# Attention and a gated MLP in one kernel: the weights' decode in 1024-column tiles with two VectorE steps, q and k in one tile of four column blocks

## The chip, the cores and the metric

The kernel runs on one core of a Trainium2 chip. A core has five engines that work side by side, each through its own queue in order: TensorE (PE, with its weight loads as PEld), VectorE (DVE), ScalarE (ACT), GpSimd (POOL) and SyncE (SP), which here only issues DMAs. SBUF is the on-chip memory with 128 partitions, PSUM the small one that TensorE writes. The metric is the device time of the program in microseconds; the kernel before was run three times, and the median counts.

## The reference, cut to what matters

```python
# q, k, v: (8, 8, 576, 64) fp32; moe weights: float64
scores = 1/sqrt(D) * q @ k.T            # a query block of 64 sees the key blocks up to its own
attn   = softmax(scores)
out    = attn @ v                       # -> x: (4608, 512), heads side by side
a = x @ w1;  b = x @ w2                 # (512, 1024) each
h = (a * b) @ w3                        # (1024, 1024)
return (h @ w_out).astype(np.float32)   # (1024, 512)
```

The four weight matrices arrive as 64-bit floats, q, k and v as 32-bit floats.

## The kernel before

The work is cut into 32 pairs of heads (8 batches with 4 pairs each, `pair(n)`, L427), each with two heads j. The matrices w3 and w_out are multiplied into one on the chip first, so that the MLP is two products, w1 and w2, a product of their results, and one more matmul. To keep fp32 accuracy at the speed of the faster 32-bit matmul format (`F32R`, a rounded float32), numbers are split into a rounded high part and a low part, and products are done in several passes: `w1h`/`w1l`, `w2h`/`w2l`, `wh`/`wl`, `xh`/`xl`, `gh`/`gl`, and for q and k `hi`/`lo`.

The program has an early stage and a late one. In the early stage the first four pairs (`EARLY`) do their attention while the weights are loaded, decoded and prepared (`gen_w`, L342). When both are done, the early pool of memory is closed and the late one opened (L480 to L486), and from there the order of TensorE's instructions is the order of the code (L488): pair 4 and the following, with MLP matmuls (`gen_moe`, L376) filled in between by the table `PLAN`. In the early stage a scheduler orders the instructions of each engine; attention's steps have the higher priority, and the letters of `EARLY_PLAN` say in which order the program offers them: S a tile of scores and its exp, V a part of the product with v, M a step of the next pair's row maximum (`shift_mask`), A and B steps of the preparation of q and k (`prep_qk`) for the next head or the own second head, N and T the end of a head and of a pair, Q the load of a later pair, and C one step of the weight generator. There are 40 C steps in the four pairs.

The decode (`load_w`, L122) turns 64-bit floats into 32-bit floats by integer arithmetic on the two 32-bit halves of each number. It works on 512 numbers per partition at a time: a DMA of 512 KB into `wraw` (5 buffers, issued on SP's queue, L130); ScalarE takes the absolute value of the high half, read with a step of two words (L135); then VectorE does four steps into `wbits` (6 buffers): a maximum (L136), a shift with a mask (L137), both on one tensor, the sign and top exponent bit merged in from the high half (L138), and the low half's top three bits merged in (L141). L138 and L141 read two tensors, one of them with a step of two words, and L141 keeps `wraw` in use to the end. There are 40 such tiles: 8 of w_out, 16 of w3 (in four-row pieces of 1 KB per partition), 8 of w1 and 8 of w2. For w1 and w2, ScalarE then rounds the result to the high part (L147) and GpSimd subtracts it for the low part (L148).

For the scores, q and k of a head are rounded on ScalarE in the early stage, on VectorE later (`cast`, L207). Two DMAs copy rounded blocks to the other 64 partitions (L209, L210), and GpSimd makes two differences of 64x576: k's low part (L211) and q's low part (L213). `lo` also holds constant rows for the mask, cast once at the start (L102), and a row of negated row maxima that a DMA writes (`shift`, L198). A score tile is two matmuls, one with `hi`, one with `lo` (L235), added up in PSUM.

Of the kernel before, what the change touches and what calls it, by code (L numbers as in the profile page):

```python
# [58 lines left out]
def block_causal_attention__then__gated_mlp_kernel(ctx, tc, qkv, consts, ident_in, w1, w2, w3t, wout, out_t):  # L59
# [43 lines left out]
    nc.gpsimd.memset(qd, 0.0)

    tl = {}
# [13 lines left out]
        tl["gh"] = pool.tile([P, NF, HALF], F32R, name="gh")  # L119
        tl["gl"] = pool.tile([P, NF, HALF], F32R, name="gl")  # L120

    def load_w(dst, src, k):  # L122

        t = tl["early"].tile([P, 1024], F32, tag="wraw", name="wraw", bufs=5)
        u = tl["early"].tile([P, 512], F32, tag="wbits", name="wbits", bufs=6)
        wide = t.bitcast(I32)
        nc.sync.dma_start(out=wide.rearrange("p (k w) -> p k w", k=k), in_=src)  # L130
# [4 lines left out]
        nc.scalar.activation(u, high.bitcast(F32), AF.Abs)  # L135
        V.tensor_scalar(out=u, in0=u, scalar1=2.0**-15, scalar2=None, op0=ALU.max)  # L136
        V.tensor_scalar(out=bits, in0=bits, scalar1=3, scalar2=0x3FFFFFF8, op0=ALU.logical_shift_left, op1=ALU.bitwise_and)  # L137
        V.scalar_tensor_tensor(out=bits, in0=high, scalar=-0x40000000, in1=bits, op0=ALU.bitwise_and, op1=ALU.bitwise_or)  # L138
        if dst is None:
            dst = u.unsqueeze(1)  # L140
        V.scalar_tensor_tensor(out=dst.bitcast(I32), in0=low.rearrange("p (k w) -> p k w", k=k), scalar=29,  # L141
                               in1=bits.rearrange("p (k w) -> p k w", k=k), op0=ALU.logical_shift_right, op1=ALU.bitwise_or)
        return u

    def load_split(dst_h, dst_l, src):
        val = load_w(None, src.unsqueeze(1), 1)
        nc.scalar.copy(dst_h, val)  # L147
        nc.gpsimd.tensor_tensor(out=dst_l, in0=val, in1=dst_h, op=ALU.subtract)  # L148

    def load_rows(dst_h, dst_l, src, c):  # L150
        for h in range(2):
            cs = slice(h * 512, (h + 1) * 512)
            load_split(dst_h[:, c, cs], dst_l[:, c, cs], src[c * P : (c + 1) * P, h * 1024 : (h + 1) * 1024])
            yield

    def cast(n, dst, src, act):
# [39 lines left out]
        yield  # L196

    def shift(n, j):  # L198
        row = lo[j][oth[j].start : oth[j].start + 1, 0, :].rearrange("p (i r) -> p i r", r=BLK)
        queue(n).dma_start(out=row.bitcast(F32), in_=ms_of[n][0:NB, j * BLK : (j + 1) * BLK].bitcast(F32))  # L200

    def prep_qk(n, j):
        rqk = raw_of[n][:, 0 : 2 * S].rearrange("p (t s) -> p t s", t=2)
        o, x = own[j], oth[j]
        if j == 1:
            shift(n, 1)
        cast(n, hi[j][o], rqk[o], CAST[0])  # L207
# [3 lines left out]
        nc.gpsimd.tensor_tensor(out=hi[j][x, 1, :], in0=rqk[o, 1, :], in1=hi[j][o, 1, :], op=ALU.subtract)  # L211
        yield
        nc.gpsimd.tensor_tensor(out=lo[j][o, 0, :], in0=rqk[o, 0, :], in1=hi[j][o, 0, :], op=ALU.subtract)  # L213
# [14 lines left out]
    def s_tile(n, j, parts, p_early):  # L228
# [3 lines left out]
        for c, q0, q1, e0 in parts:  # L232
            kr = slice(c * P, min((c + 1) * P, S))
            ks = slice(0, kr.stop - kr.start)
            for s, src in enumerate((hi[j], lo[j])):  # L235
                nc.tensor.matmul(t[ks, at : at + q1 - q0], src[:, 1, kr], src[:, 0, q0:q1], start=(s == 0), stop=(s == 1))  # L236
# [104 lines left out]

    def gen_w(wp):  # L342
        wo = tl["wo"]
        for k in range(NF):
            load_w(wo[:, k : k + 1, :], wout[k * P : (k + 1) * P, :].unsqueeze(1), 1)
            yield
        rows1 = (None for c in range(NC) for _ in load_rows(w1h, w1l, w1, c))
        pending = []

        def evacuate():  # L350
            m, acc = pending.pop(0)
            nc.scalar.copy(wh[:, m, :], acc)
            nc.vector.tensor_tensor(out=wl[:, m, :], in0=acc, in1=wh[:, m, :], op=ALU.subtract)

        for m in range(NF):
            t3 = wp.tile([P, NF, P], F32, tag="w3", name="w3", bufs=2)
            for k in range(0, NF, 4):
                src = w3t[k * P : (k + 4) * P, 2 * m * P : 2 * (m + 1) * P].rearrange("(k p) f -> p k f", p=P)
                load_w(t3[:, k : k + 4, :], src, 4)
                if k == 0:  # L360
                    yield
# [137 lines left out]
def _layout(q, k, v, moe_w1, moe_w2, moe_w3, moe_w_out):  # L499
    import numpy as np  # L500

    def heads_t(a):
# [9 lines left out]
    for c in range(4):  # L512
# [6 lines left out]
        "w1": np.ascontiguousarray(moe_w1).view(np.int64),  # L519
        "w2": np.ascontiguousarray(moe_w2).view(np.int64),  # L520
        "w3t": np.ascontiguousarray(moe_w3.T).view(np.int64),
        "wout": np.ascontiguousarray(moe_w_out).view(np.int64),
    }


# [17 lines left out]
```

## Time and profile before

| | us |
|---|---|
| three runs, median | 1022.3 |
| lowest and highest | 1020.81, 1022.79 |
| span of the profiled execution | 1019.4 |
| TensorE busy in the span | 965.8 |
| VectorE busy | 744.7 |
| GpSimd busy | 596.6 |
| ScalarE busy | 547.4 |

The span is the profiled execution's time from its first to its last instruction; what a timed run has beside it is the difference of 2.9 us between span and median. The page shows the span in 40 slices of 25.5 us with the busy share of each engine in tenths. Rows of instructions name line, engine, operation, the tile written and read, the shape, the count, then the busy time and the mean duration in ns of one, and behind the second bar the engine's idle time before them with what ended it. The row of a line or tile alone gives shortest, median and longest duration in ns.

### The profile page before, as it was taken

Reading aid. Unit: us, or ns where it says so; the run is one execution under the profiler, and the core shown is the slowest. Engines: PE = TensorE matmul, PEld = TensorE weight load, DVE = VectorE, ACT = ScalarE, POOL = GpSimd, SP = SyncE. Lnnn points to the kernel's source line nnn. Section 1 sums busy time; section 2 is a strip of 40 time slices with the busy share of each in tenths; the row PEclk is TensorE's granted clock in tenths of the full one; section 3 lists DMA queues with packets and bytes.
Section 4 is the critical chain, followed back from the end, with each engine's and each line's share of the span. In section 5 each row is a group of like instructions: output and inputs, shape, how many; then the busy total and the mean of one; then the engine's idle time right before and its main releaser. Section 6 shows DMA issues by size and latency. Waiting matters only on the chain.

```text
span 1019.4 us, 18475 instructions
## 1 busy us (share of the span) xinstructions
PE 965.8 (95%) x6594; PEld 888.3 (87%) x6624; DVE 744.7 (73%) x1320; ACT 547.4 (54%) x1433; POOL 596.6 (59%) x625
## 2 busy tenths in 40 slices
PE   3878878999999999999999999999999999999998
PEld 1444346999999999999999999999999999999998
DVE  7899886777787777777777778777777777775100
ACT  3645555656555555555565655555555556553221
POOL 3242466667676666767576767666675757673211
PEclk9889897999999999999999999999999999999999
DMA  8566542122212222222212221222222221110000
GB/s 299 170 205 196 172 122 59 49 83 61 61 51 69 73 60 73 66 78 61 84 49 84 61 66 46 70 72 64 69 67 78 60 85 48 48 25 25 1 24 24
DMA packets 37436, 80.42 MB, mean 79 GB/s; under 512 B 5408, under 2 KB 21920, under 8 KB 37344
## 3 DMA queue, kind: packets, MB, share of 16 engines
q1 hardware_dynamic: 35564, 76.26, 24.5%
q10 hardware_dynamic: 1780, 2.97, 1.2%
q8 instruction: 52, 0.85, 0.4%
q14 instruction: 40, 0.33, 0.1%
HBM read 50.76 MB, written 9.44 MB: 59 GB/s over the span
## 4 chain that ended last, share of the span: by engine, by line
PE 67%; DVE 16%; ACT 8%; issue 4%; DMA 4%; SPq 0%; ACTq 0%; POOL 0%; DVEq 0%; POOLq 0%
PE ab L387 28%; PE o L403 20%; PE s L236 7%; PE x L291 6%; DVE pl L254 5%; PE mx L183 3%; ACT ph L252 2%; ACT p L251 2%; DVE g L394 2%; PE x L275 1%; DVE wbits L138 1%; DMA wraw<-in_w 1%; DMA wraw<-in_w3t 1%; DVE wbits L136 1%; DVE x L329 1%
## 5 line engine op out<-in xcount | busy, mean ns | idle before, releaser
L257 POOL TENSOR_TENSOR rsum<-rsum,p 128x448 f32<-128x448 f32 x224 | 176.7, 789 | 108.4 <-ACT p L251 98.6
L254 DVE TENSOR_TENSOR pl<-p,ph 128x448 fp32r<-128x448 f32 x168 | 148.3, 896 | 60.1 <-ACT ph L252 59.2
L396 POOL TENSOR_TENSOR gl<-g,gh 128x288 fp32r<-128x288 f32 x128 | 107.5, 840 | 120.1 <-ACT gh L395 118.7
L395 ACT CAST gh<-g 128x288 fp32r<-128x288 f32 x128 | 55.5, 433 | 217.1 <-DVE g L394 217.1
L387 PE MATMUL ab<-xh,w2h 128*128 128x288 f32 x512 | 154.4, 301 | 0.0
L403 PE MATMUL o<-gh,wh 128*128 128x288 f32 x512 | 153.7, 300 | 0.0
L387 PE MATMUL ab<-xh,w1h 128*128 128x288 f32 x512 | 151.7, 296 | 1.6 <-ACT xh L338 1.6
L387 PE MATMUL ab<-xl,w2h 128*128 128x288 f32 x512 | 151.8, 296 | 0.0
L387 PE MATMUL ab<-xl,w1h 128*128 128x288 f32 x512 | 151.4, 296 | 0.3 <-POOL xl L339 0.3
L387 PE MATMUL ab<-xh,w2l 128*128 128x288 f32 x512 | 151.7, 296 | 0.0
L387 PE MATMUL ab<-xh,w1l 128*128 128x288 f32 x512 | 151.4, 296 | 0.0
L403 PE MATMUL o<-gl,wh 128*128 128x288 f32 x512 | 151.1, 295 | 0.0
L403 PE MATMUL o<-gh,wl 128*128 128x288 f32 x512 | 151.0, 295 | 0.0
L187 DVE TENSOR_REDUCE m<-mx 128x1 f32<-128x512 f32 (+6 forms) x320 | 128.7, 449 | 19.3 <-PE mx L183 17.4
L252 ACT ACTIVATE ph<-s 128x288 fp32r<-128x288 f32 x336 | 131.3, 393 | 0.8 <-issue 0.8
L236 PE MATMUL s<-hi 128*128 128x288 f32 (+4 forms) x384 | 123.0, 332 | 6.8 <-ACT pe L244 4.0
L211 POOL TENSOR_TENSOR hi<-raw,hi 64x576 fp32r<-64x576 f32 x64 | 92.9, 1451 | 33.3 <-ACT hi L157 16.4
L254 DVE TENSOR_TENSOR pl<-rsum,ph 128x288 fp32r<-128x288 f32 x112 | 74.6, 685 | 49.0 <-ACT ph L252 48.8
L251 ACT ACTIVATE p<-s 128x448 f32<-128x448 f32 x224 | 85.4, 381 | 46.3 <-PE s L236 43.3
L236 PE MATMUL s<-lo 128*128 128x288 f32 (+4 forms) x384 | 106.8, 306 | 3.4 <-issue 2.5
L394 DVE TENSOR_TENSOR g<-ab,a 128x288 f32<-128x288 f32 x128 | 57.7, 451 | 71.3 <-PE ab L387 63.3
L291 PE MATMUL x<-ph,vs 128*128 128x128 f32 x336 | 104.2, 320 | 0.0
(73 smaller groups left out, 2418.1 us busy)
## 6 DMA issues: line engine op xcount, KB each, us to landing
raw<-in_qkv SPq DMA_DIRECT2D x32, 896.0 KB
out_t<-o SPq DMA_DIRECT2D x64, 144.0 KB
wraw<-in_w3t SPq DMA_DIRECT2D x16, 512.0 KB
wraw<-in_w SPq DMA_DIRECT2D x16, 512.0 KB
hi<-hi SPq DMA_DIRECT2D x54, 144.0 KB
lo<-hi SPq DMA_DIRECT2D x54, 144.0 KB
wraw<-in_wout SPq DMA_DIRECT2D x8, 512.0 KB
hi<-hi ACTq DMA_DIRECT2D x10, 144.0 KB
```

What stands on the lines that cost most here:

```text
L187: nc.vector.reduce_max(m[:, col : col + 1], sc, axis=AX.X)
L211: nc.gpsimd.tensor_tensor(out=hi[j][x, 1, :], in0=rqk[o, 1, :], in1=hi[j][o, 1, :], op=ALU.subtract)
L236: nc.tensor.matmul(t[ks, at : at + q1 - q0], src[:, 1, kr], src[:, 0, q0:q1], start=(s == 0), stop=(s == 1))
L251: nc.scalar.activation(p32, t[ks, at : at + w], AF.Exp, scale=SCALE)
L252: nc.scalar.activation(ph[ks, o : o + w], t[ks, at : at + w], AF.Exp, scale=SCALE)
L254: nc.vector.tensor_tensor(out=low, in0=p32, in1=ph[ks, o : o + w], op=ALU.subtract)
L257: nc.gpsimd.tensor_tensor(out=r, in0=r, in1=p32, op=ALU.add)
L291: nc.tensor.matmul(xps[:, to : to + w], v[:, c, :], pr[:, a : a + w], start=(u < 2 and s == 0), stop=(u in (0, len(PV) - 1) and s == len(p ...
L387: nc.tensor.matmul(t[:, 0:HALF], l[:, c, fs], r, start=(c == 0 and s == 0), stop=(c == NC - 1 and s == 2))
L394: nc.vector.tensor_tensor(out=g32, in0=acc[1][:, 0:HALF], in1=a32, op=ALU.mult)
L396: nc.gpsimd.tensor_tensor(out=gl[:, f, :], in0=g32, in1=gh[:, f, :], op=ALU.subtract)
L403: nc.tensor.matmul(t[:, 0:HALF], l[:, f, es], r[:, f, :], start=(f == 0 and s == 0), stop=(f == NF - 1 and s == 2))
```

## The change

Three things are altered.

The weights are rearranged on the host so that every load is one whole tile of 1024 numbers per partition, 1 MB in one contiguous piece per partition. The 40 tiles become 20, the C steps of the table 20 instead of 40. `wraw`, the new `wy` and `wbits` have two buffers each. The decode is now: ScalarE multiplies the high half by a power of two (L134), GpSimd makes the low half's top three bits from byte 3 of each number, read as an 8-bit integer with a step of eight bytes and written as int32 (L135), and VectorE merges the sign into that (L136) and then the shifted value of ScalarE (L137). Both VectorE steps read two dense tensors, and neither reads `wraw`.

q and k of a head live in one tile `qk` of four column blocks: rounded q, rounded k, low q, low k on the head's own partitions, and constants, copied k, copied q, constants on the others. One difference of 64x1152 gives both low parts. It is on VectorE in the early stage and on GpSimd once the late pool is open. The score's two matmuls take blocks 1 and 2, then blocks 3 and 0. The two DMA copies remain.

The first load of q, k and v is cut into three DMAs, k first.

```diff
 EARLY_PLAN = (
-    "M S S S C S C C C C M S V V B C M M V A V M V M Q B M A B M N",
-    "S C C S A S S C S C V V V V V Q N T",
+    "M S S S C S C M S V V B C M M V A V M V M Q B M A B M N",
+    "S C S A S S C S V V V V V Q N T",
 )
...
-    hi = [cpool.tile([P, 2, S], F32R, name=f"hi{j}") for j in range(2)]
-    lo = [cpool.tile([P, 2, S], F32R, name=f"lo{j}") for j in range(2)]
+    qk = [cpool.tile([P, 4, S], F32R, name=f"qk{j}") for j in range(2)]
...
-        nc.sync.dma_start(out=t, in_=qkv[n // NPAIR, n % NPAIR])
+        src = qkv[n // NPAIR, n % NPAIR]
+        for cs in (slice(S, 2 * S), slice(0, S), slice(2 * S, RAW)) if n == 0 else (slice(0, RAW),):
+            nc.sync.dma_start(out=t[:, cs], in_=src[:, cs])
...
-    def load_w(dst, src, k):
-        t = tl["early"].tile([P, 1024], F32, tag="wraw", name="wraw", bufs=5)
-        u = tl["early"].tile([P, 512], F32, tag="wbits", name="wbits", bufs=6)
-        wide = t.bitcast(I32)
-        nc.sync.dma_start(out=wide.rearrange("p (k w) -> p k w", k=k), in_=src)
...
-        nc.scalar.activation(u, high.bitcast(F32), AF.Abs)
-        V.tensor_scalar(out=u, in0=u, scalar1=2.0**-15, scalar2=None, op0=ALU.max)
-        V.tensor_scalar(out=bits, in0=bits, scalar1=3, scalar2=0x3FFFFFF8, op0=ALU.logical_shift_left, op1=ALU.bitwise_and)
-        V.scalar_tensor_tensor(out=bits, in0=high, scalar=-0x40000000, in1=bits, op0=ALU.bitwise_and, op1=ALU.bitwise_or)
...
-        V.scalar_tensor_tensor(out=dst.bitcast(I32), in0=low.rearrange("p (k w) -> p k w", k=k), scalar=29,
-                               in1=bits.rearrange("p (k w) -> p k w", k=k), op0=ALU.logical_shift_right, op1=ALU.bitwise_or)
+    def load_w(dst, src):
+        t = tl["early"].tile([P, 2048], I32, tag="wraw", name="wraw", bufs=2)
+        y = tl["early"].tile([P, 1024], F32, tag="wy", name="wy", bufs=2)
+        bits = tl["early"].tile([P, 1024], I32, tag="wbits", name="wbits", bufs=2)
+        nc.sync.dma_start(out=t, in_=src)
+        high = t.rearrange("p (c two) -> p c two", two=2)[:, :, 1]
+        byte3 = t.bitcast(U8).rearrange("p (c e) -> p c e", e=8)[:, :, 3]
...
+        nc.scalar.mul(out=y, in_=high.bitcast(F32), mul=2.0**-112)
+        nc.gpsimd.tensor_scalar(out=bits, in0=byte3, scalar1=1.0 / 32, scalar2=-31.0 / 64, op0=ALU.mult, op1=ALU.add)
+        V.scalar_tensor_tensor(out=bits, in0=y.bitcast(I32), scalar=-0x80000000, in1=bits, op0=ALU.bitwise_and, op1=ALU.bitwise_or)
+        V.scalar_tensor_tensor(out=dst.bitcast(I32), in0=y.bitcast(I32), scalar=3, in1=bits, op0=ALU.logical_shift_left, op1=ALU.bitwise_or)
...
-        cast(n, hi[j][o], rqk[o], CAST[0])
+        cast(n, qk[j][o, 0:2], rqk[o], CAST[0])
         yield
-        queue(n).dma_start(out=hi[j][x, 0, :].bitcast(F32), in_=hi[j][o, 0, :].bitcast(F32))
-        queue(n).dma_start(out=lo[j][o, 1, :].bitcast(F32), in_=hi[j][o, 1, :].bitcast(F32))
-        nc.gpsimd.tensor_tensor(out=hi[j][x, 1, :], in0=rqk[o, 1, :], in1=hi[j][o, 1, :], op=ALU.subtract)
+        queue(n).dma_start(out=qk[j][x, 1, :].bitcast(F32), in_=qk[j][o, 1, :].bitcast(F32))
+        queue(n).dma_start(out=qk[j][x, 2, :].bitcast(F32), in_=qk[j][o, 0, :].bitcast(F32))
         yield
-        nc.gpsimd.tensor_tensor(out=lo[j][o, 0, :], in0=rqk[o, 0, :], in1=hi[j][o, 0, :], op=ALU.subtract)
+        (nc.gpsimd if "late" in tl else nc.vector).tensor_tensor(out=qk[j][o, 2:4], in0=rqk[o], in1=qk[j][o, 0:2], op=ALU.subtract)
         yield
...
-            for s, src in enumerate((hi[j], lo[j])):
-                nc.tensor.matmul(t[ks, at : at + q1 - q0], src[:, 1, kr], src[:, 0, q0:q1], start=(s == 0), stop=(s == 1))
+            for s, (k, q) in enumerate(((1, 2), (3, 0))):
+                nc.tensor.matmul(t[ks, at : at + q1 - q0], qk[j][:, k, kr], qk[j][:, q, q0:q1], start=(s == 0), stop=(s == 1))
```

How the rows of two engines stand before and now. First VectorE at the first tiles of w3 in the early stage (before; `w` is the decoded tile of w3; `rr` and `rb` belong to the end of pair 0):

```order
L138 SCALAR_TENSOR_TENSOR wbits<-wraw,wbits 128x512
L326 RECIPROCAL rr_154<-rr_154 128x18
L141 SCALAR_TENSOR_TENSOR w_321<-wraw,wbits 128x512
L328 STREAM_TRANSPOSE rb_368<-rr_154 128x576
L137 TENSOR_SCALAR wbits<-wbits 128x512
L136 TENSOR_SCALAR wbits<-wbits 128x512
L138 SCALAR_TENSOR_TENSOR wbits<-wraw,wbits 128x512
L137 TENSOR_SCALAR wbits<-wbits 128x512
L141 SCALAR_TENSOR_TENSOR wbits<-wraw,wbits 128x512
```

and now, at the same tiles (`m` are the row maxima of a later pair):

```order
L136 SCALAR_TENSOR_TENSOR wbits<-wy,wbits 128x1024
L180 TENSOR_TENSOR m_192<-m_192 128x1
L137 SCALAR_TENSOR_TENSOR w_286<-wy,wbits 128x1024
L136 SCALAR_TENSOR_TENSOR wbits<-wy,wbits 128x1024
L178 TENSOR_REDUCE m_390<-mx_0_391 128x1
L137 SCALAR_TENSOR_TENSOR w_356<-wy,wbits 128x1024
L136 SCALAR_TENSOR_TENSOR wbits<-wy,wbits 128x1024
L137 SCALAR_TENSOR_TENSOR wy<-wy,wbits 128x1024
L203 TENSOR_TENSOR qk_85<-raw_150,qk_85 64x1152
```

Eight steps of 512 columns have become two of twice the length for each 1024 numbers, and the difference of q and k (L203) now stands in this queue. Second GpSimd from its first work on data (before):

```order
L211 TENSOR_TENSOR hi_84<-raw_91,hi_84 64x576
L213 TENSOR_TENSOR lo_86<-raw_91,hi_84 64x576
L213 TENSOR_TENSOR lo_87<-raw_91,hi_85 64x576
L211 TENSOR_TENSOR hi_85<-raw_91,hi_85 64x576
L211 TENSOR_TENSOR hi_84<-raw_151,hi_84 64x576
L213 TENSOR_TENSOR lo_86<-raw_151,hi_84 64x576
L329 TENSOR_TENSOR x_0_153<-x_0_153,rb_368 128x576
```

and now:

```order
L135 TENSOR_SCALAR wbits<-wraw 128x1024 x8
L144 TENSOR_TENSOR w1l<-wy,w1h 128x1024
L135 TENSOR_SCALAR wbits<-wraw 128x1024
L319 TENSOR_TENSOR x_0_152<-x_0_152,rb_325 128x576
L135 TENSOR_SCALAR wbits<-wraw 128x1024
L329 TENSOR_TENSOR xl_0_329<-x_0_152,xh_0_328 128x288
```

The q/k differences have left GpSimd's queue in the early stage, and the byte steps of the weights, 20 in all, stand in their place; eight of them come ahead of its first other work.

More of the change, by code (lines that the diff above doesn't have):

```diff
@@ L11 @@
 I32 = mybir.dt.int32
+U8 = mybir.dt.uint8
 AF = mybir.ActivationFunctionType
@@ L101, in block_causal_attention__then__gated_mlp_kernel @@
     for j in range(2):
-        nc.vector.tensor_copy(lo[j][oth[j]], cst[0:D, 0 : 2 * S].rearrange("p (t s) -> p t s", t=2))
+        nc.vector.tensor_copy(qk[j][oth[j], 0:4:3, :], cst[0:D, 0 : 2 * S].rearrange("p (t s) -> p t s", t=2))
     nc.gpsimd.memset(qd, 0.0)
@@ L120, in open_late @@
         tl["gl"] = pool.tile([P, NF, HALF], F32R, name="gl")
-    def load_w(dst, src, k):
-        t = tl["early"].tile([P, 1024], F32, tag="wraw", name="wraw", bufs=5)
-        u = tl["early"].tile([P, 512], F32, tag="wbits", name="wbits", bufs=6)
-        wide = t.bitcast(I32)
-        nc.sync.dma_start(out=wide.rearrange("p (k w) -> p k w", k=k), in_=src)
-        wide = wide.rearrange("p (c two) -> p c two", two=2)
-        low, high = wide[:, :, 0], wide[:, :, 1]
-        bits = u.bitcast(I32)
-        V = nc.vector
[L135 to L141, printed above, removed]
-                               in1=bits.rearrange("p (k w) -> p k w", k=k), op0=ALU.logical_shift_right, op1=ALU.bitwise_or)
-        return u
@@ L145, in load_split @@
[L145 to L153, printed above, removed]
+    def load_w(dst, src):
[5 more added lines that the diff above has]
+        byte3 = t.bitcast(U8).rearrange("p (c e) -> p c e", e=8)[:, :, 3]
+        if dst is None:
+            dst = y
+        V = nc.vector
+        nc.scalar.mul(out=y, in_=high.bitcast(F32), mul=2.0**-112)
+        nc.gpsimd.tensor_scalar(out=bits, in0=byte3, scalar1=1.0 / 32, scalar2=-31.0 / 64, op0=ALU.mult, op1=ALU.add)
+        V.scalar_tensor_tensor(out=bits, in0=y.bitcast(I32), scalar=-0x80000000, in1=bits, op0=ALU.bitwise_and, op1=ALU.bitwise_or)
+        V.scalar_tensor_tensor(out=dst.bitcast(I32), in0=y.bitcast(I32), scalar=3, in1=bits, op0=ALU.logical_shift_left, op1=ALU.bitwise_or)
+        return y
@@ L154, in load_rows @@
+    def load_rows(dst_h, dst_l, src):
+        for c in range(NC):
+            val = load_w(None, src[c])
+            nc.scalar.copy(dst_h[:, c, :], val)
+            nc.gpsimd.tensor_tensor(out=dst_l[:, c, :], in0=val, in1=dst_h[:, c, :], op=ALU.subtract)
             yield
@@ L198, in shift @@
     def shift(n, j):
-        row = lo[j][oth[j].start : oth[j].start + 1, 0, :].rearrange("p (i r) -> p i r", r=BLK)
+        row = qk[j][oth[j].start : oth[j].start + 1, 0, :].rearrange("p (i r) -> p i r", r=BLK)
         queue(n).dma_start(out=row.bitcast(F32), in_=ms_of[n][0:NB, j * BLK : (j + 1) * BLK].bitcast(F32))
@@ L343, in gen_w @@
         wo = tl["wo"]
-        for k in range(NF):
-            load_w(wo[:, k : k + 1, :], wout[k * P : (k + 1) * P, :].unsqueeze(1), 1)
+        for u in range(NF // 2):
+            load_w(wo[:, 2 * u : 2 * u + 2, :].rearrange("p k w -> p (k w)"), wout[u])
             yield
-        rows1 = (None for c in range(NC) for _ in load_rows(w1h, w1l, w1, c))
+        rows1 = load_rows(w1h, w1l, w1)
         pending = []
@@ L356, in gen_w @@
             t3 = wp.tile([P, NF, P], F32, tag="w3", name="w3", bufs=2)
[L357 to L361, printed above, removed]
+            load_w(t3.rearrange("p k f -> p (k f)"), w3t[m])
             acc = ps_m.tile([P, 512], F32, tag="psm", name=f"w{m}")
@@ L368, in gen_w @@
             yield
-            next(rows1)
-            yield
+            if m % 2:
+                next(rows1)
+                yield
         while pending:
             evacuate()
-        for c in range(NC):
-            yield from load_rows(w2h, w2l, w2, c)
+        yield from load_rows(w2h, w2l, w2)
     def gen_moe(b):
@@ L503, in heads_t, with units @@
         return a.transpose(0, 1, 3, 2).reshape(B, NPAIR, P, S)
+    def units(w):
+        return np.ascontiguousarray(w).view(np.int64).reshape(-1, P, 1024)
     vp = np.zeros((B, NPAIR, P, 2, 5, D), v.dtype)
@@ L518, in _layout @@
         "ident": np.concatenate([np.eye(P), np.tile(np.eye(32), (4, 4))], axis=1).astype(np.float32),
[L519 to L522, printed above, removed]
+        "w1": units(moe_w1.reshape(NC, P, DF)),
+        "w2": units(moe_w2.reshape(NC, P, DF)),
+        "w3t": units(moe_w3.reshape(NF, P, NF, P).transpose(0, 3, 2, 1)),
+        "wout": units(moe_w_out.reshape(NF // 2, 2, P, DM).transpose(0, 2, 1, 3)),
     }
```

## The prediction

> **What bounds the kernel now.** I read first the slices of the page, then the busy time by stage. The page's rows show two regimes: about 170 us in which no engine is full, and then a long stretch in which TensorE is.
>
> ```profile
> PE   3878878999999999999999999999999999999998
> DVE  7899886777787777777777778777777777775100
> POOL 3242466667676666767576767666675757673211
> PEclk9889897999999999999999999999999999999999
> DMA  8566542122212222222212221222222221110000
> ```
>
> The same by stage (us of busy time, with the number of instructions):
>
> ```profile
> core 0: us, PE busy (x) PEld busy (x) DVE busy (x) ACT busy (x) POOL busy (x), PEclk, DMA share, GB/s
> 0.00:25.00 25.00, 7.27 (x23) 3.40 (x24) 18.26 (x35) 10.04 (x17) 8.77 (x11) 1.00 0.87 300
> 0.00:170.00 170.00, 124.52 (x393) 68.62 (x397) 144.63 (x255) 89.66 (x176) 70.95 (x55) 0.90 0.57 176
> 170.00:940.00 770.00, 765.08 (x5630) 743.69 (x5656) 592.73 (x1050) 440.88 (x1218) 512.14 (x555) 1.00 0.22 64
> 170.06 4.15 PE ab L387 x18
> ```
>
> The last row is from the chain in order of time: the first MLP matmul on it starts at 170.06. From there to the end of the span (1019.4) lie 849.3 us, in which TensorE is busy for 765.08 of 770. Nothing in the change takes a matmul out of that stretch, so its length stays; the time can move only by when the early stage ends. The span is 1019.4 and the median of the runs 1022.3: 2.9 us lie around the span, and I keep them.
>
> In the early stage VectorE is the fullest engine, 144.63 of 170. What fills it, by shape:
>
> ```profile
> L138 DVE SCALAR_TENSOR_TENSOR wbits<-wraw,wbits 128x512 int32<-128x512 int32 x40 | 33.3, 840 | 0.2
> L136 DVE TENSOR_SCALAR wbits<-wbits 128x512 f32<-128x512 f32 x40 | 23.8, 603 | 6.3 <-ACT wbits L135 6.2
> L137 DVE TENSOR_SCALAR wbits<-wbits 128x512 int32<-128x512 int32 x40 | 20.0, 509 | 0.1
> L141 DVE SCALAR_TENSOR_TENSOR wbits<-wraw,wbits 128x512 int32<-128x512 int32 x16 | 13.1, 824 | 0.1
> L141 DVE SCALAR_TENSOR_TENSOR w<-wraw,wbits 128x512 int32<-128x512 int32 x16 | 12.4, 776 | 0.0
> L141 DVE SCALAR_TENSOR_TENSOR wo<-wraw,wbits 128x512 int32<-128x512 int32 x8 | 6.5, 823 | 0.0
> ```
>
> These six rows sum to 109.1 us: the decode of the weights, 160 instructions. It waits for almost nothing (at most 6.3 us before L136), so its own length is what counts. But the means are not the price of the step. The timeline shows the price twice, without and with GpSimd at work:
>
> ```profile
> 129.73 0.69 DVE L138 SCALAR_TENSOR_TENSOR wbits<-wraw,wbits 128x512 int32<-128x512 int32 x1
> 131.01 4.64 POOL L148 TENSOR_TENSOR w2l<-wbits,w2h 128x512 fp32r<-128x512 f32 x3 [6.77 <-ACT w2h L147]
> 131.06 1.77 DVE L141 SCALAR_TENSOR_TENSOR wbits<-wraw,wbits 128x512 int32<-128x512 int32 x1
> 132.75 1.76 DVE L138 SCALAR_TENSOR_TENSOR wbits<-wraw,wbits 128x512 int32<-128x512 int32 x1
> 134.44 1.50 DVE L136 TENSOR_SCALAR wbits<-wbits 128x512 f32<-128x512 f32 x1
> 136.46 0.41 DVE L137 TENSOR_SCALAR wbits<-wbits 128x512 int32<-128x512 int32 x1
> ```
>
> While three GpSimd subtractions ran (131.01 to 135.65), VectorE finished one step for each of them, 1.5 to 1.8 us instead of 0.41 or 0.69. Alone, the 160 steps would take 40 x (0.69 + 0.69 + 0.41 + 0.41) = 88.0 us; so 21 us of the 109.1 are waiting for GpSimd.
>
> **The change, part by part.** *Decode on VectorE.* Removed: 109.1 us. Added: 20 tiles x 2 steps of 1024 columns. The growth per column comes from two reductions, which read one after the other 512 and 256 columns:
>
> ```profile
> L187 DVE TENSOR_REDUCE m<-mx 128x1 f32<-128x512 f32 x10 | 6.7, 680 | 0.4 <-PE mx L183 0.4
> L187 DVE TENSOR_REDUCE m<-mx 128x1 f32<-128x256 f32 x5 | 2.1, 417 | 0.2 <-PE mx L183 0.2
> ```
>
> (680 - 417)/256 = 1.03 ns a column, so a step of 1024 costs 0.69 + 512 x 1.03 ns = 1.22 us alone, and 40 of them 48.8 us.
>
> *The q/k difference.* In the early stage nine differences of 64x1152 are on VectorE (pairs 0 to 3, and the first head of pair 4): 0.69 + 640 x 1.03 ns = 1.35 us each, 12.1 us. They leave GpSimd:
>
> ```profile
> L213 POOL TENSOR_TENSOR lo<-raw,hi 64x576 fp32r<-64x576 f32 x10 | 16.0, 1603 | 6.3 <-issue 5.3 <-POOL w1l L148 0.4
> L211 POOL TENSOR_TENSOR hi<-raw,hi 64x576 fp32r<-64x576 f32 x10 | 15.9, 1585 | 29.3 <-ACT hi L157 16.4 <-issue 8.2 <-DVE hi L157 4.3
> L148 POOL TENSOR_TENSOR w1l<-wbits,w1h 128x512 fp32r<-128x512 f32 x8 | 14.3, 1790 | 30.2 <-ACT w1h L147 29.0 <-issue 1.1
> L148 POOL TENSOR_TENSOR w2l<-wbits,w2h 128x512 fp32r<-128x512 f32 x8 | 11.9, 1505 | 12.8 <-ACT w2h L147 12.7
> L148 POOL TENSOR_TENSOR w1l<-wbits,w1h x8: 1269/1520/2948, 53.8 to 122.8; 128x512 fp32r<-128x512 f32 x8
> L103 POOL MEMSET qd<- 128x1152 bf16 x1 | 1.1, 1057 | 0.3 <-POOLq L531 0.3
> ```
>
> So GpSimd loses 31.9 us, less one double difference that stays (the second head of pair 4, about 3 us).
>
> *The new GpSimd step* (byte 3 of every weight, eight bytes apart, scaled and rounded to int32, 1024 columns) has no row. It reads one tensor. Below it lies the memset, which reads none: 1057 ns for 1152, hence 0.94 us for 1024. Above it lies the subtraction, which reads two: the fastest takes 1269 ns for 512, hence 2.5 us. I take the middle, 1.7 us; 20 of them are 34 us. GpSimd then does 34 + 26.2 (L148, whose 16 halves become 8 wholes) + 3, where it did 31.9 + 26.2; its few other steps stay. So GpSimd's load hardly changes (+5), and with it the 21 us that VectorE loses to it: I keep 20, since VectorE's exposed work is smaller (61 us for 88) and the load larger; between the ends 0.94 and 2.5, 16 to 26.
>
> [...]
>
> VectorE: -109.1 + 48.8 + 12.1 + 20 = -28.2 us. By rows its stage sum is 144.63 as a union; scaled to the rest, 144.6 - 28.2 x 0.92 (union over row sum; neighbours overlap by some 0.09 us) = 118.6. If its idle time (170 - 144.6 = 25.4) stays, the stage ends at 144.
>
> *TensorE becomes next.* It is busy for 124.52 of the 170, of which only 7.27 lie in the first 25 us; behind that it has 117.2 us in 145, a share of 81%. Its work there is not changed. With the share at 90% and the clock as granted (0.90) the stage ends at 25 + 130 = 155; with the clock at 1.00 and a share of 95%, near 25 + 111 = 136. Between VectorE's 144 and TensorE's 155 I take 149.
>
> *Nothing for ScalarE:* 89.66 us in 170, and 20 strided steps of 1024 for 40 of 512 pay fewer starts. *Nothing for the load's split in three:* q and k arrive earlier, the constants and the first weights two issues later on SP's queue; I set 0, between -2 and +1 us. *Nothing for the DMA of the weights:* the same bytes, in longer runs; but five half-size buffers become two whole ones, and SP's queue stands at a weight load until ScalarE and GpSimd have both read the tile two before it, with the next q/k/v load queued behind. Loads were late already:
>
> ```profile
> L135 ACT ACTIVATE wbits<-wraw 128x512 f32<-128x512 f32 x40 | 25.9, 671 | 22.0 <-DMA wraw<-in_w 11.1 <-DMA wraw<-in_w3t 7.5 <-DMA wraw<-in_wout 1.7
> 58.51 7.42 DMA wraw<-in_w3t
> 8.89 0.67 ACT L135 ACTIVATE wbits<-wraw 128x512 f32<-128x512 f32 x1 [0.32 <-DMA wraw<-in_wout]
> ```
>
> 20.3 us of ScalarE's waiting is for them. An earlier release works against fewer buffers; 0, from -5 to +10 us.
>
> *Late stage.* One GpSimd difference for two, and both score matmuls read the same tile. The slack is there:
>
> ```profile
> 406.98 0.76 DVE L157 CAST hi<-raw 64x1152 fp32r<-64x1152 f32 x1
> 410.18 1.43 POOL L213 TENSOR_TENSOR lo<-raw,hi 64x576 fp32r<-64x576 f32 x1
> 415.61 0.30 PE L236 MATMUL s<-hi 128*128 128x288 f32 x1
> ```
>
> The difference ends at 411.6, the matmul starts at 415.61: 4 us cover it, and one longer step must not use them up. 0, between -1 and +3 us over the stretch. If the cover failed by 1 us for each of 54 heads it would cost 54 us, but nothing makes the one step longer than the two together, 2.9 us.
>
> Sum: 149 + 849.3 + 2.9 = 1001 us.
>
> **The rivals.** *The access that VectorE and GpSimd share is the bound* (chance 0.15). If the two never overlap, their steps alone add up: now 88.0 + 20 x 1.40 + 16 x 1.27 = 136 us and some 10 of small steps, nearly the stage. The 1.40 is the short end of L211:
>
> ```profile
> L211 POOL TENSOR_TENSOR hi<-raw,hi x2: 1398/1653/1908, 6.7 to 12.4; 64x576 fp32r<-64x576 f32 x2
> ```
>
> Afterwards 60.9 + 34 + 20.3 + 2.8 = 118 and the same 10: 18 us less, hence 1004. For it speaks the stretch at 131; against it that there VectorE's 3 steps and GpSimd's 3 (5.6 us alone) took 4.9 together. [...]
>
> *Other waits take over* (0.20): weight loads two deep, or the attention's own round of exp, PV and masks, hold the stage at 158 to 170. Then 1010 to 1022. The 7.42 us load on the chain speaks for it; that VectorE is busy 144.63 of 170 against.
>
> *TensorE follows at once* (0.09): the stage ends near 136 or before, clock 1.00; 982 to 988.
>
> *GpSimd becomes the bound* (0.12), the slower side. The first weights are there at 8.89 (the row above), and the last decode step starts 11 us before the stage ends:
>
> ```profile
> L141 DVE SCALAR_TENSOR_TENSOR wbits<-wraw,wbits x16: 633/686/1771, 51.2 to 159.1; 128x512 int32<-128x512 int32 x16
> ```
>
> Between the two lie 150 us for GpSimd's queue. Beside the byte steps it holds 39 us: 26.2 + 3 + some 10 of the 12.8 that are left of its 70.95. If a byte step costs more than (150 - 39)/20 = 5.5 us, the queue is longer than today's stage, and VectorE's steps wait for each of them. At 6 us: 9 + 159 + 11 = 179, that is 1031. The point is twice the row that reads two tensors; no row has byte input or a conversion to int32, which is all that speaks for it.
>
> *That the decode does not come down to two VectorE steps* is excluded by the order: 40 such steps stand there.
>
> **How the numbers follow.** My own case (0.44) has 990 to 1010 with 1001 as its middle. A difference of 0.2%, 2 us, is about what a measurement of this kernel can tell. Faster by more: 0.44 + 0.15 + 0.09 + 0.15 of the 0.20 = 0.83; same: the last 0.05 of that rival; slower: 0.12. The range leaves out most of the slower case and half of the deepest: 984 to 1021.
>
> **What would show it.** Right: the two new VectorE steps at 1.2 us alone and below 1.9 in the mean, GpSimd's byte step between 0.94 and 2.5 us, the first MLP matmul near 149 us, and 849 us behind it. Wrong: a byte step over 5.5 us with VectorE idle before its own steps; TensorE waiting for weights with VectorE idle and the loads late; or the stretch behind the first MLP matmul other than 849 by more than 3 us.

## The result, and the profile after

The changed kernel takes 1009.4 us (four runs, 1008.27 to 1011.10), the kernel before, run beside it, 1022.4 (1020.81 to 1022.79): a ratio of 0.9877, 95% interval 0.9863 to 0.9891. That is 13 us faster, where 21 were forecast (1001.0, range 984 to 1021). The profiled execution took 1009.86 us with a span of 1008.1.

The slices of the page after, in the columns of before:

```profile
PE   1889888999999999999999999999999999999998
DVE  5876757777777877777777777877777777775100
POOL 2374437757576767666675657666666666573211
PEclk9999899999999999999999999999999999999999
DMA  9674422222212212222222122212212222110000
```

VectorE has become emptier in five of the first six slices (the second shows an 8 in both), and TensorE is full from the eighth on, as before. Where the change shows is the length of the early stage. On the chain of waits the first long run of MLP matmuls, at 170.06 before, now stands here:

```profile
160.27 2.90 PE ab L373 x18
```

The chain does not pick the same matmul in both kernels, so I take one that both have, the first product with v of pair 4. Before, in the timeline:

```profile
174.38 0.41 PE L291 MATMUL x<-ph,vs 128*128 128x128 f32 x1
```

and after:

```profile
163.33 0.41 PE L281 MATMUL x<-ph,vs 128*128 128x128 f32 x1
```

It comes 11.05 us earlier; from it to the end of the span lie 845.0 us before (1019.4 - 174.38) and 844.8 after (1008.1 - 163.33). So the whole gain is in the early stage, and the late one has not moved.

The early stage falls into three parts: the head up to the first matmul of the weights' product (w3 times w_out), the product up to its last matmul, and a tail that is mostly attention (the last decode steps of w2 still start in it, up to 159.1 us before and 132.4 after). Busy time by part (PE, PEld, DVE, ACT, POOL, then granted clock, DMA share, GB/s), before:

```profile
0.00:42.60 42.60, 21.20 (x72) 12.82 (x72) 33.48 (x65) 20.20 (x39) 12.36 (x13) 0.92 0.74 247
42.60:141.50 98.90, 85.68 (x251) 43.67 (x252) 90.28 (x157) 52.46 (x101) 38.22 (x26) 0.91 0.59 178
141.50:170.10 28.60, 17.74 (x73) 12.23 (x73) 20.97 (x33) 17.09 (x38) 20.47 (x17) 0.83 0.24 64
```

and after:

```profile
0.00:42.30 42.30, 17.73 (x68) 10.49 (x68) 27.41 (x42) 20.48 (x33) 10.46 (x13) 1.00 0.81 272
42.30:130.20 87.90, 80.41 (x235) 40.73 (x235) 64.71 (x74) 47.86 (x76) 48.58 (x27) 0.92 0.55 189
130.20:160.30 30.10, 21.54 (x96) 15.12 (x96) 19.14 (x30) 18.36 (x40) 11.79 (x9) 0.90 0.28 81
```

Only the product became shorter, by 11.0 us. In it VectorE went from 91% busy to 74%, TensorE from 87% to 91%. Head and tail, 72 us together, are as long as they were.

VectorE's decode and q/k rows of the stage after:

```profile
L136 DVE SCALAR_TENSOR_TENSOR wbits<-wy,wbits 128x1024 int32<-128x1024 int32 x20 | 25.3, 1268 | 13.8 <-ACT wy L134 7.2 <-POOL wbits L135 6.6
L203 DVE TENSOR_TENSOR qk<-raw,qk 64x1152 fp32r<-64x1152 f32 x9 | 14.9, 1652 | 1.7 <-ACT qk L148 1.6
L137 DVE SCALAR_TENSOR_TENSOR w<-wy,wbits 128x1024 int32<-128x1024 int32 x8 | 13.5, 1692 | 2.5 <-PE w L350 2.4
L137 DVE SCALAR_TENSOR_TENSOR wy<-wy,wbits 128x1024 int32<-128x1024 int32 x8 | 11.7, 1464 | 0.2
L137 DVE SCALAR_TENSOR_TENSOR wo<-wy,wbits 128x1024 int32<-128x1024 int32 x4 | 4.8, 1224 | 0.1
```

The decode is 25.3 + 13.5 + 11.7 + 4.8 = 55.3 us where it was 109.1, less than the 68.8 forecast. GpSimd's new step, as the row of its line has it (shortest, median and longest in ns, first and last start):

```profile
L135 POOL TENSOR_SCALAR wbits<-wraw x20: 1096/1176/2200, 11.6 to 124.4; 128x1024 int32<-128x1024 uint8 x20
```

So VectorE lost more work than forecast, and the gain in time was smaller. What holds the stage at 160, if it is not VectorE?

### The profile page after: what moved, and what is told of

It is laid out like the page before. It is cut to its first block, busy times and chain, and to the rows that moved or that the text cites. A ratio compares the mean times of both kernels' runs of the same rounds, so it can differ in the third digit from the quotient of the medians.

```text
span 1008.1 us, 18157 instructions
## 1 busy us (share of the span) xinstructions
PE 959.4 (95%) x6624; PEld 884.4 (88%) x6624; DVE 699.3 (69%) x1209; ACT 544.3 (54%) x1405; POOL 586.4 (58%) x564
## 4 chain that ended last, share of the span: by engine, by line
PE 63%; DVE 19%; ACT 9%; issue 5%; POOL 2%; DMA 2%; DVEq 0%; ACTq 0%; POOLq 0%
PE ab L373 25%; PE o L389 20%; DVE pl L244 7%; PE s L226 7%; PE x L281 4%; PE mx L174 3%; DVE g L380 2%; PE w L350 2%; ACT p L241 2%; ACT ph L242 2%; DVE m L178 2%; PE x L265 1%; DVE x L319 1%; DMA qk<-qk 1%; DVE wbits L136 1%
## 5 line engine op out<-in xcount | busy, mean ns | idle before, releaser
L226 PE MATMUL s<-qk 128*128 128x288 f32 (+4 forms) x768 | 159.6, 315 | 14.8 <-DMA qk<-qk 8.9
L203 POOL TENSOR_TENSOR qk<-raw,qk 64x1152 fp32r<-64x1152 f32 x55 | 146.9, 2671 | 2.4 <-POOL vs L216 0.4
L226 PEld LDWEIGHTS s<-qk 128*128 128x128 f32 (+1 forms) x768 | 116.6, 184 | 28.2 <-issue 14.5
L244 DVE TENSOR_TENSOR pl<-rsum,ph 128x288 fp32r<-128x288 f32 x112 | 66.8, 597 | 48.8 <-ACT ph L242 47.0
```

What stands on the lines that cost most here:

```text
L203: (nc.gpsimd if "late" in tl else nc.vector).tensor_tensor(out=qk[j][o, 2:4], in0=rqk[o], in1=qk[j][o, 0:2], op=ALU.subtract)
L226: nc.tensor.matmul(t[ks, at : at + q1 - q0], qk[j][:, k, kr], qk[j][:, q, q0:q1], start=(s == 0), stop=(s == 1))
L244: nc.vector.tensor_tensor(out=low, in0=p32, in1=ph[ks, o : o + w], op=ALU.subtract)
```

## The experiments

Theory A, the prediction's: VectorE's queue still sets the stage. Theory B: TensorE's queue does, with the product in it. Theory C, the prediction's rival: the attention's own round of exp, PV, masks and copies. Theory D: the loads, two deep.

| kernel | us | ratio to before (95%) | product, first to last matmul | MLP on the chain | VectorE busy | TensorE busy |
|---|---|---|---|---|---|---|
| before | 1022.4 | | 42.6 to 141.5 | 170.06 | 144.7 | 124.6 |
| changed | 1009.4 | 0.9877 (0.9863 to 0.9891) | 42.3 to 130.2 | 160.27 | 111.3 | 119.7 |
| decode alone | 1015.4 | 0.9928 (0.9912 to 0.9944) | 40.1 to 132.9 | 164.42 | 109.2 | 122.7 |
| q/k alone | 1016.6 | 0.9941 (0.9925 to 0.9957) | 41.8 to 137.3 | 166.68 | 142.6 | 123.2 |
| VectorE cut | 1008.8 | 0.9863 (0.9837 to 0.9889) | 39.9 to 130.2 | 158.92 | 70.0 | 119.1 |
| product cut | 998.2 | 0.9764 (0.9742 to 0.9785) | 42.0 to 103.9 | 148.00 | 119.2 | 82.4 |
| both cut | 994.3 | 0.9726 (0.9704 to 0.9748) | 40.3 to 103.3 | 146.19 | 78.0 | 78.9 |
| VectorE more | 1022.8 | 1.0015 (1.0003 to 1.0028) | 47.7 to 135.1 | 173.69 | 142.2 | 123.0 |
| product more | 1012.8 | 0.9911 (0.9895 to 0.9927) | 42.0 to 134.2 | 163.11 | 112.3 | 129.2 |
| weights on ACT's queue | 1011.2 | 0.9881 (0.9848 to 0.9913) | 39.8 to 126.0 | 160.81 | 113.0 | 122.2 |
| steps later | 1010.8 | 0.9892 (0.9856 to 0.9928) | 44.5 to 138.0 | 160.89 | 109.7 | 121.7 |
| one first load | 1007.6 | 0.9853 (0.9832 to 0.9873) | 40.4 to 128.2 | 158.22 | 112.1 | 119.1 |
| changed, again | 1009.9 | 0.9875 (0.9861 to 0.9890) | 41.2 to 128.0 | 158.05 | 111.0 | 119.1 |
| one first load, again | 1008.4 | 0.9863 (0.9850 to 0.9877) | 41.6 to 128.9 | 158.95 | 113.0 | 120.8 |

Busy times are those of the early stage, in us. All columns behind the ratio come from one profiled execution each. The two profiles of the changed kernel differ by 2.2 us in where the product and the stage end, so a shift of that size in these columns says nothing.

### The two halves of the change

Decode alone is the changed kernel with the old q/k lines:

```diff
-        (nc.gpsimd if "late" in tl else nc.vector).tensor_tensor(out=qk[j][o, 2:4], in0=rqk[o], in1=qk[j][o, 0:2], op=ALU.subtract)
+        nc.gpsimd.tensor_tensor(out=hi[j][x, 1, :], in0=rqk[o, 1, :], in1=hi[j][o, 1, :], op=ALU.subtract)
...
+        nc.gpsimd.tensor_tensor(out=lo[j][o, 0, :], in0=rqk[o, 0, :], in1=hi[j][o, 0, :], op=ALU.subtract)
```

> The new decode alone; q and k as before (two tiles, two GpSimd differences of 64x576 a head, one first load). If VectorE's sum sets the end of the early stage, as the prediction had it: VectorE is rid of nine differences of 1.65 us (14.9 us), so up to 14 us below the changed kernel's 1009.4, 996 to 1003. If the waits around the first head (q/k copies, 3.4 us later in the changed kernel) and the attention's own round set it: 1003 to 1008. If the change to q and k is what brings part of the gain (GpSimd relieved of 29 us): 1012 to 1020.

> The old decode; q and k in four column blocks, one difference a head (on VectorE in the early stage), first load in three. If VectorE's sum sets the stage, it gains 12 to 15 us of differences and loses some 10 of waiting for GpSimd: 1022 to 1027. If only the head of the program counts (second passes of the first scores 3.4 us later): 1025 to 1026. If the relief of GpSimd is worth something: below 1020.

Measured: 1015.4 and 1016.6, that is 7.4 and 6.3 below the kernel before, run beside them (1022.9). Together that is 13.7, where the whole change brought 13. The decode is worth only half of the gain; the expectation's third case held, not the first. The q/k part was forecast to cost VectorE 12.1 us. In the q/k-alone kernel the rows of VectorE's old decode and of the difference are:

```profile
L139 DVE SCALAR_TENSOR_TENSOR wbits<-wraw,wbits 128x512 int32<-128x512 int32 x40 | 29.9, 754 | 0.2
L137 DVE TENSOR_SCALAR wbits<-wbits 128x512 f32<-128x512 f32 x40 | 20.1, 509 | 0.6 <-ACT wbits L136 0.5
L138 DVE TENSOR_SCALAR wbits<-wbits 128x512 int32<-128x512 int32 x40 | 18.9, 480 | 0.2
L142 DVE SCALAR_TENSOR_TENSOR w<-wraw,wbits 128x512 int32<-128x512 int32 x16 | 12.6, 792 | 0.0
L213 DVE TENSOR_TENSOR qk<-raw,qk 64x1152 fp32r<-64x1152 f32 x9 | 12.2, 1351 | 2.4 <-ACT qk L158 2.2
L142 DVE SCALAR_TENSOR_TENSOR wbits<-wraw,wbits 128x512 int32<-128x512 int32 x16 | 11.3, 705 | 0.1
...
L142 DVE SCALAR_TENSOR_TENSOR wo<-wraw,wbits 128x512 int32<-128x512 int32 x8 | 5.3, 677 | 0.0
```

The decode's six rows sum to 98.1 us where they were 109.1, without a change of their own: with nine double differences moved off GpSimd these steps became 11.0 us shorter, for 12.2 us of new work on VectorE. VectorE is as full as before (142.6 and 144.7), and still the kernel is 6 us faster. So this half's gain is not VectorE's work; which wait it shortened, these runs don't settle.

### Less work for VectorE, for TensorE, for both

VectorE cut:

```diff
-        V.scalar_tensor_tensor(out=bits, in0=y.bitcast(I32), scalar=-0x80000000, in1=bits, op0=ALU.bitwise_and, op1=ALU.bitwise_or)
+        V.scalar_tensor_tensor(out=bits[:, n8], in0=y.bitcast(I32)[:, n8], scalar=-0x80000000, in1=bits[:, n8], op0=ALU.bitwise_and, op1=ALU.bitwise_or)
```

with `n8 = slice(0, 8)`, and the second step likewise; GpSimd clears the tiles that stay empty once at the start, and the tiles of w3 are two fixed ones.

> The changed kernel with both VectorE decode steps 8 columns wide in place of 1024, so that 36 to 52 us of VectorE's work in the early stage are gone and all other steps, loads and waits stay; the weights are not decoded, so the output is not the reference's. VectorE still the bound: the stage ends 25 to 45 us earlier, 965 to 985. TensorE or the attention's own round the bound: 1002 to 1010. Weight loads two deep the bound: 1007 to 1010, since each tile still goes through all its buffers.

Measured: 1008.8, the time of the changed kernel, and the product lies where it lay:

```profile
39.90:130.20 90.30, 83.60 (x246) 42.19 (x247) 33.92 (x75) 52.34 (x82) 44.27 (x29) 0.92 0.57 198
```

VectorE is busy for 33.9 of these 90.3 us. Theory A falls for the changed kernel: 41 us less of VectorE's work buy nothing. The time lies in two of the recorded cases, the one of TensorE or attention's round and the one of the loads, so those three stay.

Product cut (seven of the eight matmuls of each of the eight blocks are left out, 112 of 128 recorded ones):

```diff
-            for k in range(NF):
-                nc.tensor.matmul(acc, t3[:, k, :], wo[:, k, :], start=(k == 0), stop=(k == NF - 1))
+            for k in range(1):
+                nc.tensor.matmul(acc, t3[:, k, :], wo[:, k, :], start=True, stop=True)
```

> The changed kernel with one of the eight matmuls of each block of the weights' product (56 of 64 blocks' matmuls left out, so the output is not the reference's): some 49 us of TensorE's 118 in the early stage are gone and the weights' tiles come free as soon as their first matmul is done. TensorE's in-order queue the bound: 20 to 45 us earlier, 965 to 990. VectorE the bound: 1005 to 1010. The attention's own round or the loads the bound: 1003 to 1010.

Measured: 998.2. That is 11 us less than the changed kernel for 48 us of matmuls (one starts every 0.43 us), between what B and what A and C expected. The stretch of the product is 26 us shorter, but the attention that is left behind it is 14 longer:

```profile
42.00:103.90 61.90, 39.71 (x126) 22.88 (x128) 54.89 (x65) 38.74 (x67) 33.61 (x20) 0.75 0.63 215
103.90:148.00 44.10, 25.37 (x89) 16.57 (x89) 35.92 (x38) 27.34 (x50) 26.48 (x15) 0.67 0.39 126
```

Both cut at once:

> Both cuts at once: VectorE decode steps of 8 columns and one of eight matmuls of the weights' product; the output is not the reference's. What is left is the attention's own round with the loads, ScalarE's and GpSimd's steps of the decode. If behind TensorE's product (998.2 with that cut alone) VectorE is next: 980 to 990. If the attention's own round or the loads are next: 994 to 999.

Measured: 994.3. With VectorE and TensorE each at little more than half of the stage (78.0 and 78.9 of 146.2), the stage is only 14 us shorter than in the changed kernel. No engine is full then; the chain of this kernel shows what is left:

```profile
7.03 9.13 DMA qk<-qk
...
59.53 7.76 DMA qk<-qk
...
90.49 7.34 DMA qk<-qk
...
121.78 7.69 DMA qk<-qk
...
146.19 3.00 PE ab L378 x18
```

Four waits for the copies of q and k to the other partitions, 31.9 us of 146.2, the last three some 31 us apart. Beside the copies of 144 KB the 1 MB weight loads move (DMA share 0.68 in the product's stretch). So what is left is theory C or D, attention's own round or the loads: the recorded case that held names both, and this kernel still has all loads and the decode's steps on ScalarE and GpSimd.

Nor does this chain carry over to the changed kernel as it stands. These are TensorE's waits for the copies in the early stage (total us, times, longest), first in the changed kernel, then with both cuts:

```profile
PE s L226 <- DMA qk<-qk: 8.9, 1, 8.9
PE s L227 <- DMA qk<-qk: 22.2, 4, 9.3
```

In the changed kernel TensorE waits for a copy once, in the head; the other waits appear when its work is taken away.

### More work for VectorE and for TensorE

VectorE more (the first step twice), product more (the first two matmuls of each block twice):

```diff
+        for _ in range(2):
+            V.scalar_tensor_tensor(out=bits, in0=y.bitcast(I32), scalar=-0x80000000, in1=bits, op0=ALU.bitwise_and, op1=ALU.bitwise_or)
...
+            for i, k in enumerate((0, 1, 0, 1, 2, 3, 4, 5, 6, 7)):
```

> The changed kernel with the first VectorE step of the decode done twice in each of the 20 tiles (the second time changes nothing in the result): 20 x 1.22 = 24.4 us more for VectorE, which is then as full as it was with 33 us more before the change. If VectorE has that much slack now: 1008 to 1012. If its queue sets the stage: 1025 to 1034.

> The changed kernel with ten matmuls for eight in each block of the weights' product (the first two are done twice, the result is the same): 32 more recorded matmuls, one every 0.43 us, 13.8 us more for TensorE between its first and its last matmul of the product. If TensorE is what fills that stretch: 1020 to 1024. If VectorE's or the attention's round sets it: 1009 to 1014.

The changed kernel once more, beside them:

> The changed kernel once more, beside the next three. Every theory: 1007 to 1011.

Measured: the changed kernel again 1009.9 (ratio 0.9875, 0.9861 to 0.9890); VectorE more 1022.8, 12.9 above it, between the two cases; product more 1012.8, only 2.9 above it, the second case. The doubled step came to 55.3 us where the single one took 25.3, so VectorE got 30 us more and not the expected 24.4. VectorE more, by part (this execution took 1025.85, 3 us above the median):

```profile
0.00:47.70 47.70, 21.35 (x79) 12.95 (x80) 35.77 (x48) 23.26 (x40) 10.65 (x13) 0.98 0.77 262
47.70:135.10 87.40, 77.20 (x222) 38.01 (x223) 82.15 (x82) 42.32 (x66) 44.88 (x24) 0.93 0.53 179
135.10:173.70 38.60, 24.45 (x96) 17.02 (x96) 24.29 (x34) 20.82 (x42) 17.88 (x12) 0.80 0.22 62
```

VectorE is 94% busy in the product's stretch, as it was before the change (91%), and the stage has about its old length (173.7 for 170.1). The loss does not lie in that stretch (87.4 for 87.9) but on both sides: the first tiles must be decoded before the first matmul (5.4 us later), and the tail is 8.5 us longer. Two facts together: with VectorE at 142 to 145 us the stage takes 167 to 174 (before, q/k alone, VectorE more), with VectorE at 110 to 113 or at 70 it takes 158 to 161, TensorE's work being the same. Decode alone is the exception: 164.4 with VectorE at 109.2, but GpSimd, which has both the differences and the byte steps there, is busy for 96.7 us (70.8 in the changed kernel). All this fits VectorE as the main bound before, which stopped being it somewhere on the way down; the kernel before was not itself run with less work on VectorE alone.

Product more, its middle part:

```profile
42.00:134.20 92.20, 90.24 (x263) 44.98 (x266) 68.85 (x75) 48.77 (x77) 47.06 (x28) 0.98 0.52 180
```

13.8 us of matmuls lengthened the stretch by 4.3: TensorE's idle time in it fell from 7.5 to 2.0 us, and the granted clock was higher (0.98 for 0.92). So TensorE was not the whole limit of that stretch either.

### The head and the order of the steps

> The changed kernel with the first two weight loads issued on ScalarE's queue, behind the copies of q and k, instead of on SP's queue ahead of them. If the 1 MB weight tiles in front of the copies are what makes the first scores late (second pass of the first scores at 26.65 in the changed kernel): they run near 20, and if the whole stage shifts with the head, the time is 1003 to 1006. If the head's delay is made up later behind the weights' product: 1008 to 1010. If the weights, now later, set the stage: 1011 to 1016.

```diff
-        nc.sync.dma_start(out=t, in_=src)
+        (nc.scalar if len(first) < 2 else nc.sync).dma_start(out=t, in_=src)
```

> The changed kernel with the 20 weight steps spread over the four early pairs as 3, 5, 6, 6 instead of 5 each, so that the last matmuls of the weights' product stand in pair 3 and not in pair 2. If part of the faster decode is given back because the attention of pair 3 then runs alone, with TensorE waiting for it: 1003 to 1007. If TensorE's total load or VectorE's sets the stage: 1008 to 1011. If the later weights make the stage wait for the last of them: 1011 to 1016.

```diff
-                for step in (EARLY_PLAN if early else PLAN)[j].split():
+                for step in (EARLY_PLAN[n] if early else PLAN)[j].split():
```

The table has one row pair for each early pair then, with 3, 5, 6 and 7 letters C (one more than there are steps; the last one has nothing left to do).

Measured: 1011.2 and 1010.8, both the changed kernel's time within their intervals. With the first weights behind the copies the product starts 2.5 us earlier and ends 4.2 earlier (1.4 and 2.0 against the second profile), and the MLP starts no earlier (160.81): the tail grew to 34.8 us. With the steps later the product ends 7.8 later, and the MLP again starts at the same time (160.89): the tail shrank to 22.9. So the moment at which the product ends does not set the end of the stage. That is no case against B as a whole, for TensorE's queue holds the same work in all of these (119 to 122 us busy): 1010.8 lies in the recorded case of TensorE's total load or VectorE's, 1008 to 1011. For the weights behind the copies none of the cases fits: the second pass of the first scores came at 23.62, not near 20, and 1011.2 lies where the weights were to come too late, though the product ended early.

Taken together: A falls for the changed kernel. Of B, 48 us of TensorE's work are worth 11. With VectorE emptied as well, 146 of the 160 us stay, and these runs do not part attention's round (C) from the loads (D) in them.

> The changed kernel with the first load of q, k and v in one DMA, as before. The prediction set the split at 0, between -2 and +1. If the split only changes when q and k arrive: 1009 to 1011, the split is worth up to 2. If it is the split that puts the first two score matmuls ahead of the second half of the row maxima in TensorE's queue, so that these wait for the copies: without it the second pass of the scores runs at 23 to 24 instead of 26.65, 1006 to 1009.

```diff
-        for cs in (slice(S, 2 * S), slice(0, S), slice(2 * S, RAW)) if n == 0 else (slice(0, RAW),):
-            nc.sync.dma_start(out=t[:, cs], in_=src[:, cs])
+        nc.sync.dma_start(out=t, in_=qkv[n // NPAIR, n % NPAIR])
```

> The changed kernel with the first load of q, k and v in one DMA, timed again beside the changed kernel. If the split is what costs its 2 us at the head of the program: 1.5 to 2.5 below the changed kernel, 1006 to 1008.5. If the first measurement was scatter: within 1 of it.

Measured: 1007.6, and again 1008.4 (ratio 0.9863, 0.9850 to 0.9877) beside the changed kernel's 1009.9 (0.9875, 0.9861 to 0.9890). It was lower both times, by 1.5 to 1.8, but the intervals overlap: not settled, and at most 2 us. What the split does is seen in the timeline. In the changed kernel:

```profile
15.78 0.82 PE L226 MATMUL s<-qk 128*128 128x288 f32 x2 [8.86 <-DMA qk<-qk]
16.40 1.08 PE L174 MATMUL mx<-kb,qd 128*128 128x448 bf16 x4
26.65 0.85 PE L226 MATMUL s<-qk 128*128 128x288 f32 x2 [5.27 <-DMA qk<-ms]
```

The first two score matmuls stand in TensorE's queue ahead of four of the six groups of row maxima (mx) and wait there for the copies; the maxima behind them, and with them the scores' second pass, come late. Before, with four of the six groups ahead of the scores, it was

```profile
12.67 0.83 PE L236 MATMUL s<-hi 128*128 128x288 f32 x2
23.26 0.82 PE L236 MATMUL s<-lo 128*128 128x288 f32 x2 [2.54 <-issue]
```

so the second pass has come 3.4 us later. With one load it is at 24.78, and in the second measurement at 23.59 against 25.55: the split accounts for some 2 us of it, not for all.

## Why the prediction was right in sign and 8.4 us too low

**What bounded the kernel before: borne out in the main.** VectorE given back 30 us takes the kernel to 1022.8, its old time. But q/k alone gained 6.3 us with VectorE as full as before, so VectorE was not the whole of it.

**The decode on VectorE: right, its loss to GpSimd too large.** The new step alone was forecast at 1.22 us; the undisturbed ones took 1.224. The 20 us lost to GpSimd were 55.3 - 48.8 = 6.5. Beside a byte step that was under way before it, a VectorE step took 2.04 us where the undisturbed ones took 1.22:

```profile
46.23 1.38 POOL L135 TENSOR_SCALAR wbits<-wraw 128x1024 int32<-128x1024 uint8 x1 [1.82 <-DMA wraw<-in_w3t]
46.66 2.04 DVE L137 SCALAR_TENSOR_TENSOR wy<-wy,wbits 128x1024 int32<-128x1024 int32 x1
```

But only nine of the 40 steps took more than 1.3 us; the 20 was carried over from a kernel with 160 steps.

**The q/k difference: mis-sized.** 14.9 us for 12.1 on VectorE, but the half as a whole gained 6.3 us, where the sum had it as pure cost. VectorE's other steps became 11 us shorter in it, a relief that the sum had hidden in the one figure of 20; that leaves VectorE as full as before, so it does not by itself explain the gain.

**GpSimd's byte step: right.** 1.42 us in the mean (28.3 in 20), 1.10 alone, between 0.94 and 2.5 and far from the 5.5 at which GpSimd would have become the bound.

**"If its idle time stays, the stage ends at 144", "between VectorE's 144 and TensorE's 155 I take 149": this step failed.** The stage ended at 160.27 (158.05 in the second profile). VectorE's sum of rows fell by 39 us, not 28, and its idle time did not stay at 25.4: 160.3 - 111.3 = 49. And of two limits the later one counts, not their middle: 155 at least. Nor did the 155 hold: TensorE's share was 91% in the product's stretch, as I had set it for the whole stage, but 72% in the 30 us of the tail, and 85% from 25 us on. Luck hid a part of this: with the 39 us that VectorE lost in fact, the same working would have put VectorE's end at 134 and the middle with 155 at some 145, hence 997. The loss to GpSimd set too high brought the forecast 4 us nearer.

**The rival "other waits take over": it came nearest, and which wait is open.** The stage of 160 lies in its 158 to 170, the time 0.6 us below its 1010 to 1022. The weights are decoded earlier, but with VectorE and TensorE both emptied the stage still ends at 146. Whether attention's round or the loads two deep hold it there was not tried: no run gave the changed kernel more buffers, and only the first two loads were moved. The loads are late in the changed kernel too:

```profile
L135 POOL TENSOR_SCALAR wbits<-wraw 128x1024 int32<-128x1024 uint8 x20 | 28.3, 1416 | 58.2 <-DMA wraw<-in_wout 12.5 <-DMA wraw<-in_w3t 11.9 <-DMA wraw<-in_w 11.0
```

GpSimd waits 35.4 us for them before its byte steps.

**The shared access of VectorE and GpSimd as the bound: no.** It would have moved with VectorE's work, and the cut of 41 us moved nothing. That a step of one engine can take longer beside one of the other still shows in single steps, as in the 2.04 us for 1.22 above, and the 11 us by which VectorE's steps became shorter in q/k alone fit it. What the two engines share there, no run shows.

**TensorE at once (982 to 988): no**; the stage ended at 160, not near 136.

**The load's split and the head, 0: nearly.** The second pass is 3.4 us later, some 2 of them by the split, the product starts as early as before (42.3 and 42.6), and at most 2 us of time hang on it. **The late stage, 0: right**, 844.8 for 845.0.

**What lies around the span:** 1.8 us (1009.86 - 1008.1), not 2.9. The 2.9 was the difference between a median and the span of another execution. In sum: 11.3 (160.3 for 149) - 1.5 (the 849.3 was counted from another matmul of the chain; it is 847.8) - 1.1 = 8.7, and 1001.2 + 8.7 is the 1009.9 of the profiled run.

## What to carry to other kernels

The fullest engine of a stage is worth its excess over the next limit, not its whole saving: take the later of the two limits, and look for a third one in the stretches where no engine is full (here the 72 us of head and tail, which the change left as long as they were). A change that takes work from a bound engine should be tried from both sides, with that engine emptied and with the work put back. Here emptying it further gave 0.6 us and putting 30 back cost 12.9, which shows the knee that one run alone would not. Where an end does not move when the work before it ends 2 to 4 us earlier or 8 later, the moment at which that work ends does not set it; its amount still can, as the cut product shows. And a wait that stands on the chain of a kernel with its work cut out is not thereby one of the kernel itself: look for it there too.

## What the runs showed of the hardware

In the product's stretch the granted clock followed TensorE's share of the time: 0.98 at a share of 98% (product more), 0.92 at 91% (changed) and 0.75 at 64% (product cut). The product's own matmuls took 632 ns in the mean at 0.92 and 814 at 0.75, here in the changed kernel and with the product cut:

```profile
L350 PE MATMUL w<-wo,w 128*128 128x512 f32 x128 | 62.3, 632 | 0.2 <-DVE w L137 0.2
L350 PE MATMUL w<-wo,w 128*128 128x512 f32 x16 | 11.6, 814 | 6.9 <-DVE w L137 6.8
```

That may be part of why 48 us less of TensorE's work bought only 11 and 13.8 more cost only 3; it was not worked out. In the head the clock did not follow the share: the profile of the changed kernel gives 1.00 there at a share of 42%. What sets the clock, these runs don't show.

In the kernel with both cuts a copy of q and k of 144 KB was on the chain for 7.3 to 9.1 us each time. The DMA packets in that trace, taken in order with 64 to a copy, show where that time goes. The copies issued at 56.00, 140.84 and 141.41 us, with no load moving, had their first packet 1.2 to 1.3 us after the issue and their last 2.0 to 2.1 us after it. Of the other 17, issued beside loads, 15 had their first packet only 3.9 to 5.7 us after the issue and their last 5.8 to 8.4 us after it; the remaining two took 2.3 and 2.4 us. So in this trace a copy beside loads mostly waited to begin. What less of that would be worth to the time was not tried.
